# A scheduler that knows transfer rates and TensorE's clock, an urgency for every operation, and q in 64-row tokens

## The chip, the cores and the metric

The kernel runs on one core of one Trainium2 chip. The metric is the device time of one execution in microseconds (us); times are medians over runs of the same program. All arithmetic is on 32-bit floats (the MLP's matmuls take operands split into a high and a low part).

## The reference

One block: an adaptive layer norm, a gated long convolution, and a squared-ReLU MLP. S = 2048 tokens, D = 640 channels, F = 1728 hidden units.

```
mod = silu(c) @ w_mod                      # six rows of D: sa, ca, ga, sb, cb, gb
h  = layernorm(q) * (1 + ca) + sa
kv = causal_conv4(k, shift_k) * v          # 4 taps per channel
y  = causal_conv(kv, ssm_k) + kv * ssm_D   # 2048 taps per channel, by FFT
x  = q + ga * h * y
h  = layernorm(x) * (1 + cb) + sb
out = x + gb * (relu(h @ w1 + b1) ** 2 @ w2 + b2)
```

## The kernel before

**Two stages.** The first computes x, channel by channel, in NB = 5 batches of 128 channels. The second is the MLP over NC = 8 token tiles of 256 tokens.

**A batch b of the first stage.** `kv_load` brings k and v in (eight loads of 256 KB, written into tiles of KV), `kv` transposes them on TensorE, applies the four taps, multiplies, and stores kv to DRAM (`kv_d<-KV`); it is read back in another layout (`load_x`, `p<-kv_d`), beside ssm_k (`load_h`, `p<-in_A_ssm_k_dram`). The long convolution is a two-step Fourier transform by matmuls: `unit_a` (64x64 matmuls with the constant cw, `ps<-cst,p`), `spectra` (with the constant gb, `ps<-a,gb`), a complex product on DVE and POOL (`front`, tiles wx), `back` (with the constant gi), and `unit_y` (transposes, then the constant ca). In batch 0 the spectra of ssm_k are computed first (`early_h`). The epilogue of a batch is `load_xp` (q for these channels), `prep` (the norm of q, on ACT, DVE and POOL), and `finish`: tokens of MLP tiles 0 and 1 stay in SBUF, the others are summed on POOL and stored to DRAM (`x_d<-xp`). Statistics of q over all 640 channels are needed before the first epilogue: `q_stats` loads all of q once more, `stats1_end` finishes them. The modulation rows come from w_mod (25 loads, `wm<-in_w_mod_dram`, scaled on ACT and summed on POOL).

**The second stage.** Per token tile: load x (`load_x1`), statistics (`stats2`), normalise (`prep_hat`), transpose and split (`prep_xt`), then 14 blocks of F with `mlp_front` (x times w1), `mlp_middle` (bias, ReLU, square, split) and `mlp_back` (times w2, accumulated in four PSUM banks), and `mlp_out`. The weights are loaded once, during tile 0 and before (`w_load`: load, copy of the high part on ACT, low part on DVE).

**Token layout.** A partition of the first stage's result holds 16 neighbouring tokens: token = 64 n + 16 c + l lies at partition 32 c + n. So q's loads (`qsrc`) and the output's stores (`osrc`) go by four groups of 32 partitions.

**Who sets the order.** Nothing runs as written. Every operation becomes a node of a graph (`Graph`) with an engine, a cost in us, and the buffers it uses; nodes that belong together share a key, such as ("kn", 4) for batch 4's k and v loads. `levels` gives each node a priority: the longest path from it to the end plus a bias from the table `BIAS`, by kind or by kind and batch. `order` then plays the run forward: at each moment every engine takes the ready node of highest priority whose buffers are free, and a buffer is placed where it first fits. What comes out is one fixed order per engine, which `emit` writes down and `keep_order` pins. Loads and stores go out on SP's queue; `sp_issue` makes each wait for the fourth before it (OUT = 4), so that at most four are in flight. A DMA's time in the plan is `moved`: bytes per run of contiguous memory, one rate for all.

In the trace every operation recorded through the graph has line L375, and every SP load or store L564.

Of the kernel before, what the change touches and what calls it, by code (L numbers as in the profile page):

```python
# [13 lines left out]
AF = mybir.ActivationFunctionType  # L14
# [3 lines left out]
P = 128  # L18
# [5 lines left out]
NC = S // CH  # L24
EPS = 1e-5
OUT = 4

# [77 lines left out]


class Node:
    __slots__ = ("engine", "calls", "cost", "deps", "bufs", "entries", "dma", "id", "next", "prio", "key", "lock")  # L110


class Graph:
    def __init__(self):
        self.nodes, self.group, self.bufs = [], None, []
        self.key, self.bias = ("", 0), {}

    def buf(self, name, shape, dtype, choices, cell=32, line=None, psum=False):

# [85 lines left out]
    def order(self, lag=0.06, pelag=0.1, patience=0.0, trace=None):  # L205
# [55 lines left out]

        ready = {e: [] for e in ("PE", "ACT", "DVE", "POOL", "SP")}
        free = dict.fromkeys(ready, 0.0)
        soon = {e: [] for e in ready}
        need = [len(n.deps) for n in nodes]
        when = [0.0] * len(nodes)
        events = []
# [12 lines left out]
        while done < len(nodes):  # L280
            moved = False
            for e in ready:
                while free[e] <= t + 1e-9:
# [9 lines left out]
                            break  # L293
                    if pick is None:
                        break
                    if patience and e == "PE":
                        wait = [w for w, pr2, j in soon[e] if t < w < t + patience and pr2 < pr]
                        if wait:
                            heapq.heappush(events, (min(wait), -1))
                            break  # L300
                    n = nodes[ready[e].pop(pick)[1]]
                    for b, ci in got:
                        taken[b.n] = ci
                        for s in b.choices[ci][0]:
                            owner[s] = b.n
                    end = t + n.cost
                    if n.lock:
                        port = (end, e)
                    if e == "PE":
# [2 lines left out]
                            end = max(end, block + 4.0)  # L312
                            block, ent = end, ent - 256
                    if n.dma:
                        start = max(t + 1.4, dma_free)
                        dma_free = start + n.dma
                        land = dma_free + 0.7
                        heapq.heappush(events, (land, -1))
                        if e == "SP":
                            landed.append(land)  # L320
                        free[e] = t + n.cost
                        end = land
                    else:
                        free[e] = end
# [4 lines left out]
                    for i in n.next:  # L329
                        l = 0.0 if nodes[i].engine == e and not n.dma else pelag if e == "PE" else lag  # L330
                        when[i] = max(when[i], end + l)
                        need[i] -= 1
                        if not need[i]:
                            heapq.heappush(events, (when[i], i))
                            if patience:
                                soon[nodes[i].engine].append((when[i], -nodes[i].prio, i))
# [13 lines left out]
            while events and events[0][0] <= t + 1e-9:  # L350
                _, i = heapq.heappop(events)
                if i >= 0:
                    n = nodes[i]
                    bisect.insort(ready[n.engine], (-n.prio, i))
                    if patience:
                        soon[n.engine] = [x for x in soon[n.engine] if x[2] != i]
# [21 lines left out]
def _constants():  # L378
# [17 lines left out]
    for mm in range(1, 32):  # L396
# [27 lines left out]
    gt[0, :, 0] = gi.reshape(2, 64, 128).transpose(1, 0, 2)  # L424
    return {
        "cw": cw.astype(f),
        "ca": np.kron(np.eye(2), ca).astype(f),
        "gb": gb.reshape(128, 4096).astype(f),
        "gi": gt.reshape(128, 64, 2, 2, 16).swapaxes(3, 4).reshape(128, 4096).astype(f),
    }  # L430


# [1 line left out]
def ssm_mlp_kernel(  # L434
# [135 lines left out]
    def moved(o, i, run):  # L570
        x = o if isinstance(o, View) and o.ap is None else i
        n = (x.p[1] - x.p[0]) * x.ix.size * 4
        return n / run * (0.0095 + 4.1e-5 * run) / 16

    def sp_dma(o, i, run):
        g.add("SP", 0.4, (sp_issue, "dma", (o, i), {}), [x for x in (o,) if isinstance(x, View)],
              [x for x in (i,) if isinstance(x, View)], dma=moved(o, i, run))

    def act_dma(o, i, run):
        g.add("ACT", 0.06, (nc.scalar.dma_start, "dma", (o, i), {}), [x for x in (o,) if isinstance(x, View)],  # L580
              [x for x in (i,) if isinstance(x, View)], dma=moved(o, i, run))

    def cost(engine, op, args, kw):
# [89 lines left out]
    def mod_sum(j):  # L673
        ts = []
        for b in range(NB):
            t = stg(f"wm_{j}_{b}")
            ts.append(t)
            g.key = ("lm", j)
            sp_dma(t, w_mod[b * P : (b + 1) * P, j * D : (j + 1) * D], 2560)
            g.key = ("ms", j)  # L680
            act.activation(t, t, AF.Copy, scale=sg[:, b : b + 1])
            if b:
                add(pool, ts[0], ts[0], t)
        return ts[0]
# [34 lines left out]
    def q_stats(choices, l0, n, line=None):  # L719
        g.key = ("lq", l0)  # L720
        t = sbuf(f"q_{l0}", (P, n, D), choices, line=line)
        for a in range(4):
            sp_dma(t[32 * a : 32 * a + 32], qsrc[a, :, l0 : l0 + n], 2560)
        g.key = ("st1", l0)
        for i in range(n):
            dve_stats(st1[:, l0 + i], t[:, i])

    def stats1_end():
        g.key = ("st1e", 0)
        act.activation(rs1, st1[:, :, 1], AF.Sqrt, bias=eps_t)  # L730
        dve.reciprocal(rs1, rs1)
        dve.scalar_tensor_tensor(nm1, st1[:, :, 0], -1.0, rs1, op0=ALU.mult, op1=ALU.mult)


    gb = sbuf("gb", (P, 16, 2, 2, 64), [whole("S5")])
# [221 lines left out]
    def load_xp(b):  # L957
        g.key = ("lxp", b)
        t = XPt[b] = sbuf(f"xp_{b}", (P, NL, P), [whole(f"XP{b % 2}")])
        for a in range(4):  # L960
            sp_dma(t[32 * a : 32 * a + 32], qsrc[a, :, :, b * P : (b + 1) * P], 512)

    def prep(b, j):
        g.key = ("pra", b)
# [2 lines left out]
        u = U[b, j] = sbuf(f"u_{b}_{j}", (P, 4, P), UT if b < 2 else UT + up0 + up1 if b < NB - 1 else up0)  # L967
        for i in range(4):
            l = 4 * j + i
            act.activation(u[:, i], XPt[b][:, l], AF.Identity, scale=rs1[:, l : l + 1], bias=nm1[:, l : l + 1])  # L970
# [182 lines left out]
    def mlp_out(n):  # L1153
        g.key = ("out", n)
        for s in range(2):
# [7 lines left out]
            for i in range(2):  # L1163
                o = slice(i * 320, (i + 1) * 320)
                add(dve if s else pool, X1t[n][:, s, o], t[:, o], X1t[n][:, s, o])
                if s or i:
                    o = o if s else slice(0, D)
                    for a in range(4):
                        (act_dma if a % 2 else sp_dma)(
                            osrc[a, :, 2 * n + s, o], X1t[n][32 * a : 32 * a + 32, s, o], 2560  # L1170
                        )
        if n < NC - 1:
            for a in range(4):
                sp_dma(osrc[a, :, 2 * n : 2 * n + 2], X1t[n][32 * a : 32 * a + 32], 5120)

    BIAS = {
        "b1": 40, ("comb", 3): 40, "f2": -170, "fin": -160, ("fin", 0): -10, "gate": -185, "h": 40,
        ("h", 1): 215, "hat": 155, ("kn", 4): -25, ("ks", 0): 10, "kst": 335, ("kt", 3): 95, ("kt", 4): 60,
        ("lh", 3): -10, ("lh", 4): -15, ("lm", 1): 20, ("lm", 3): 40, ("mr", 1): -40, ("mr", 2): 15,
        ("mr", 4): 160, "mul": 40, ("mul", 2): 100, ("pa", 1): 60, "pac": -5, ("pac", 1): -55, ("pac", 2): 5,  # L1180
        ("pac", 3): 190, ("prm", 0): 40, "prp": -130, "qp": 490, ("qpc", 0): -5, ("st1", 10): 205, "tc": 225,
        ("vt", 2): -105, "wl": -240, ("wl", 6): -130, ("wl", 7): -85, ("x", 0): -10, "xt": 610, "y": -40,
        ("y", 0): -85, ("yc", 1): 90, ("yc", 4): 55,
    }

    KVB, PAB, XB, QB = ANY[::-1], ANY, ANY, ANY[2:6][::-1]
# [169 lines left out]
```

## Time and profile before

| | |
|---|---|
| median of three runs | 708.71 us (706.67 to 709.03) |
| the profiled execution | 712.65 us |
| its span, first to last instruction | 710.9 us |
| mean granted TensorE clock | 0.973 |
| PE busy | 650.5 us, 92% of the span |
| DVE, ACT, POOL busy | 381.3, 328.6, 253.1 us |
| moved by DMA | 74.46 MB |

The profile is of one execution, and its times are read against its own 712.65 us. A busy TensorE is not TensorE at its peak: a matmul at half clock counts as busy for twice as long. The engine that waits is not always the one that is late: a row names what released it.

### The profile page before, as it was taken

The numbers are of one execution on the slowest core, as the hardware profiler recorded it, in microseconds if no ns is written. First come the engines' busy times: TensorE is split into PE (matmuls) and PEld (weight loads), VectorE is DVE, ScalarE is ACT, GpSimd is POOL, SyncE is SP. The second block draws the span as 40 slices with busy tenths as digits, with TensorE's granted clock in tenths as the row PEclk, the third lists the DMA queues.
The fourth block names the chain that finished last, engine by engine and source line by source line (L and its number), as shares of the span: only waits on it lengthen the run. The fifth ranks groups of instructions, "written<-read, shape, count | busy, mean of one in ns | idle before, by whom it ended". The sixth has DMA issues, their size and how long they took to land.

```text
span 710.9 us, 17833 instructions
## 1 busy us (share of the span) xinstructions
PE 650.5 (92%) x7509; PEld 581.9 (82%) x7509; DVE 381.3 (54%) x780; ACT 328.6 (46%) x678; POOL 253.1 (36%) x316
## 2 busy tenths in 40 slices
PE   4968989789996899799999999999999999999996
PEld 3857867667785596479999999999999998998996
DVE  4545365567686667685235537456255356254451
ACT  3544657658877688465323324324124224233330
POOL 1126576336878287625401301203004004013010
PEclk9799999989998899999999999999999999999999
DMA  9888799799775761743002002001020020020011
GB/s 211 259 226 268 199 244 255 193 201 235 166 205 145 184 135 47 235 142 104 0 1 75 1 1 75 1 19 56 1 49 27 1 69 7 1 75 0 1 38 38
DMA packets 109125, 74.46 MB, mean 105 GB/s; under 512 B 49267, under 2 KB 96371, under 8 KB 108789
## 3 DMA queue, kind: packets, MB, share of 16 engines
q1 hardware_dynamic: 107088, 72.87, 39.2%
q8 instruction: 59, 0.97, 0.6%
q10 hardware_dynamic: 1892, 0.44, 0.3%
q14 instruction: 22, 0.17, 0.1%
q0 software_dynamic: 64, 0.01, 0.0%
HBM read 58.88 MB, written 14.42 MB: 103 GB/s over the span
## 4 chain that ended last, share of the span: by engine, by line
PE 69%; DMA 20%; DVE 5%; issue 2%; ACT 1%; SPq 1%; POOL 0%; DVEq 0%; ACTq 0%; POOLq 0%
PE ps L375 69%; DMA wm<-in_w_mod_dram 4%; DMA q<-in_A_q_dram 2%; DMA KV<-in_A_k_dram 2%; DMA kv_d<-KV 2%; DMA gb<-in_gb_dram 2%; DMA p<-kv_d 2%; DMA w2s<-in_B_w_dram 1%; DVE mtmp L375 1%; SPq L564 1%; DMA xp<-in_A_q_dram 1%; DVE KV L375 1%; DMA p<-in_A_ssm_k_dram 1%; DMA KV<-in_A_v_dram 1%; DVE s L375 1%
## 5 line engine op out<-in xcount | busy, mean ns | idle before, releaser
L375 PE MATMUL ps<-xt,w_S 128*128 128x512 f32 (+1 forms) x935 | 161.2, 328 | 0.9 <-ACT mtmp L375 0.9
L375 PEld LDWEIGHTS ps<-xt,w_S 128*128 128x128 f32 x935 | 139.2, 189 | 16.7 <-ACT mtmp L375 1.3
L375 PE MATMUL ps<-w_S,hring 128*128 128x320 f32 x648 | 106.3, 311 | 0.0
L375 PEld LDWEIGHTS ps<-w_S,hring 128*128 128x128 f32 x648 | 97.6, 188 | 0.7
L375 PE MATMUL ps<-a,gb 128*64 128x128 f32 x1280 | 81.8, 283 | 5.0 <-issue 1.3
L375 PEld LDWEIGHTS ps<-a,gb 128*64 128x64 f32 x1280 | 72.7, 141 | 14.6 <-issue 6.8
L375 ACT ACTIVATE hring<-mtmp 128x256 fp32r<-128x256 f32 x74 | 30.7, 416 | 112.2 <-PE ps L375 110.1
L375 POOL TENSOR_TENSOR x<-mtmp,x 128x640 f32<-128x640 f32 (+1 forms) x9 | 13.5, 1501 | 188.9 <-DVE mtmp L375 188.9
L375 ACT ACTIVATE mtmp<-ps,b1t 128x256 f32<-128x256 f32 (+1 forms) x112 | 51.8, 472 | 49.8 <-DVE hring L375 21.6
L375 POOL TENSOR_TENSOR wx<-wx 128x256 f32<-128x256 f32 x80 | 60.6, 777 | 25.5 <-DVE wx L375 23.5
L375 PE MATMUL ps<-cst,p 64*64 64x64 f32 x2560 | 51.4, 236 | 16.2 <-issue 8.3
L375 PEld LDWEIGHTS ps<-cst,p 64*64 64x64 f32 x2560 | 46.8, 149 | 21.3 <-issue 10.6
L375 DVE TENSOR_TENSOR hring<-mtmp,hring 128x256 fp32r<-128x256 f32 x74 | 34.1, 469 | 55.4 <-ACT hring L375 55.2
L375 DVE TENSOR_TENSOR mtmp<-ps,mtmp 128x256 f32<-128x256 f32 (+1 forms) x99 | 41.2, 420 | 39.6 <-ACT mtmp L375 39.5
L375 ACT ACTIVATE a<-ps 128x512 f32<-128x512 f32 x80 | 44.9, 629 | 25.7 <-PE ps L375 25.6
L375 POOL TENSOR_TENSOR x<-x,gb2row 128x640 f32<-128x640 f32 x16 | 25.1, 1586 | 82.7 <-ACT mtmp L375 51.9
L375 DVE TENSOR_TENSOR wx<-ps,wx 128x512 f32<-128x512 f32 x64 | 41.0, 684 | 24.3 <-PE ps L375 18.9
L375 PE MATMUL ps<-w_S,w_W 128*128 128x320 f32 x312 | 52.4, 311 | 0.3 <-DVE w_W L375 0.3
L375 ACT ACTIVATE w_W<-mtmp 128x256 fp32r<-128x256 f32 (+1 forms) x38 | 15.8, 417 | 71.5 <-PE ps L375 71.3
L375 PEld LDWEIGHTS ps<-w_S,w_W 128*128 128x128 f32 x312 | 47.0, 188 | 0.9 <-DVE w_W L375 0.5
L375 PE MATMUL ps<-gi,wx 64*128 64x128 f32 x640 | 41.0, 278 | 3.5 <-ACT q L375 3.3
L375 DVE SCALAR_TENSOR_TENSOR mtmp<-mtmp 128x256 f32<-128x256 f32 x91 | 42.8, 471 | 2.4
(128 smaller groups left out, 1031.7 us busy)
## 6 DMA issues: line engine op xcount, KB each, us to landing
wm<-in_w_mod_dram SPq DMA_DIRECT2D x25, 320.0 KB, 4.7
KV<-in_A_k_dram SPq DMA_DIRECT2D x20, 256.0 KB, 4.2
KV<-in_A_v_dram SPq DMA_DIRECT2D x20, 256.0 KB, 4.5
p<-in_A_ssm_k_dram SPq DMA_DIRECT2D x20, 256.0 KB, 4.6
p<-kv_d SPq DMA_DIRECT2D x20, 256.0 KB, 4.7
xp<-in_A_q_dram SPq DMA_DIRECT2D x20, 256.0 KB, 5.4
out_dram<-x SPq DMA_DIRECT2D x28, 160.0 KB, 2.6
w1s<-in_B_w_dram SPq DMA_DIRECT2D x13, 320.0 KB, 3.9
```

Of the source, the lines that this page charges most:

```text
L375: fn(*real, **{k: a.real() if isinstance(a, View) else a for k, a in kw.items()})
L564: nc.sync.dma_start(o, i)
```

## The change

Four things.

1. **The plan's rates.** `order` gives TensorE a clock that follows its own use: time is cut in windows of 10.24/3 us (from `phase`, 0), a window runs at half rate if the one before was used too little. DMAs get a rate by kind (`moved`: a factor 1.4 for transfers of at most 32 partitions and for those whose destination is in DRAM, 1.05 for the others), 1.2 us before and 1.0 us after the transfer instead of 1.4 and 0.7; a DMA issued on ACT costs ACT 0.4 us. The unused `patience` goes.
2. **An urgency per operation.** `BIAS` goes. A table `URGE` gives each node a number by its key and its turn within the key; the number takes the place of the path length. It covers the whole first stage, the weights, and token tiles 0 and 1. Nodes without an entry (token tiles 2 to 7) keep their path length, less 3000, without any bias.
3. **Tokens by 64 partitions.** token = 32 m + 16 h + l lies at partition 64 h + m. q's loads and the output's stores go by two groups of 64 partitions; the second of a batch's two q loads is issued on ACT's queue; the constants ca and gi are permuted to match.
4. **q's statistics by whole rows.** Partition p loads its 16 tokens 16 p to 16 p + 15, two at a time, over all 128 partitions (9 loads instead of 24). Two matmuls with every second column of the identity bring the statistics into the token layout.

```diff
-            n.prio = level[n.id] + self.bias.get(n.key[0], 0.0) + self.bias.get(n.key, 0.0)
+            n.prio = level[n.id]
+        turn = {}
+        for n in nodes:
+            i = n.nth = turn.get(n.key, 0)
+            turn[n.key] = i + 1
+            table = self.urge.get(n.key, ())
+            if i < len(table):
+                n.prio = table[i] / 10
+            elif self.urge:
+                n.prio -= 3000.0
...
+        def rate(k):
+            if k not in slow:
+                if k < 4:
+                    slow[k] = False
+                else:
+                    before = rate(k - 1) == 0.5
+                    u = util.get(k - 1, 0.0) / WINDOW
+                    slow[k] = u < 0.85 if before else u < 0.45
+            return 0.5 if slow[k] else 1.0
...
-                    end = t + n.cost
+                    end = run(t, n.cost) if e == "PE" else t + n.cost
...
-                        start = max(t + 1.4, dma_free)
+                        start = max(t + 1.2, dma_free)
                         dma_free = start + n.dma
-                        land = dma_free + 0.7
+                        land = dma_free + 1.0
...
-        return n / run * (0.0095 + 4.1e-5 * run) / 16
+        few = x.p[1] - x.p[0] <= 32
+        away = not isinstance(o, View) or o.ap is not None
+        return n / run * (0.0095 + 4.1e-5 * run) / 16 * (1.4 if few or away else 1.05)
...
-    qsrc = q.rearrange("(n c l) d -> c n l d", n=32, c=4)
-    osrc = out.rearrange("(n c l) d -> c n l d", n=32, c=4)
+    qsrc = q.rearrange("(m h l) d -> h m l d", m=64, h=2)
+    osrc = out.rearrange("(m h l) d -> h m l d", m=64, h=2)
+    qrow = q.rearrange("(p l) d -> p l d", p=P)
...
-        for a in range(4):
-            sp_dma(t[32 * a : 32 * a + 32], qsrc[a, :, l0 : l0 + n], 2560)
+        for i in range(0, n, 2):
+            e = min(i + 2, n)
+            sp_dma(t[:, i:e], qrow[:, l0 + i : l0 + e], 2560 * (e - i))
...
+        t = psum("stp", (P, NL, 2), ONE)
+        with g.as_one(0.3):
+            for h in range(2):
+                mm(t[64 * h : 64 * h + 64].rearrange("p l c -> p (l c)"), ident[:, h::2], st1.rearrange("p l c -> p (l c)"), True, True)
-        act.activation(rs1, st1[:, :, 1], AF.Sqrt, bias=eps_t)
+        act.activation(rs1, t[:, :, 1], AF.Sqrt, bias=eps_t)
...
-        for a in range(4):
-            sp_dma(t[32 * a : 32 * a + 32], qsrc[a, :, :, b * P : (b + 1) * P], 512)
+        for h in range(2):
+            (act_dma if h else sp_dma)(t[64 * h : 64 * h + 64], qsrc[h, :, :, b * P : (b + 1) * P], 512)
...
-            for a in range(4):
-                sp_dma(osrc[a, :, 2 * n : 2 * n + 2], X1t[n][32 * a : 32 * a + 32], 5120)
-    BIAS = {
-        "b1": 40, ("comb", 3): 40, "f2": -170, "fin": -160, ("fin", 0): -10, "gate": -185, "h": 40,
...
+            for a in range(2):
+                sp_dma(osrc[a, :, 2 * n : 2 * n + 2], X1t[n][64 * a : 64 * a + 64], 5120)
+    URGE = {
+        ("kn", 0): [-144, -133, -123, -113, -179, -226, -17, -154],
...
+        ("kn", 4): [-1541, -1530, -1561, -1582, -1692, -1743, -1753, -1823],
...
+        ("lh", 0): [-189, -229, -84, -129, -56, -102, -4, -54],
...
+        ("lq", 0): [-809, -777],
...
+        ("lq", 12): [-530, -962],
...
+        ("lw", 0): [-1602, -1764],
...
+        ("mul", 3): [-1807, -1814, -1827, -1820, -1878, -1865, -1894, -1901, -1922, -1915, -1953, -1960, -2042,
+            -2049, -2080, -2087],
...
-    g.bias = BIAS
+    g.urge = URGE
```

More of the change, by code (lines that the diff above doesn't have):

```diff
@@ L109 @@
 class Node:
-    __slots__ = ("engine", "calls", "cost", "deps", "bufs", "entries", "dma", "id", "next", "prio", "key", "lock")
+    __slots__ = ("engine", "calls", "cost", "deps", "bufs", "entries", "dma", "id", "next", "prio", "key", "lock", "nth")
 class Graph:
@@ L202, in levels, with order, run @@
             level[n.id] = top + n.cost + n.dma
-            n.prio = level[n.id] + self.bias.get(n.key[0], 0.0) + self.bias.get(n.key, 0.0)
-    def order(self, lag=0.06, pelag=0.1, patience=0.0, trace=None):
-        self.levels()
+            n.prio = level[n.id]
[8 more added lines that the diff above has]
+                n.prio -= 3000.0
+    def order(self, lag=0.06, pelag=0.1, phase=0.0):
+        self.levels()
+        util, slow = {}, {}
+        def rate(k):
[7 more added lines that the diff above has]
+            return 0.5 if slow[k] else 1.0
+        def run(t, work):
+            while work > 1e-9:
+                k = int((t + phase) / WINDOW)
+                for j in range(len(slow), k):
+                    rate(j)
+                room = (k + 1) * WINDOW - phase - t
+                r = rate(k)
+                step = min(room, work / r)
+                util[k] = util.get(k, 0.0) + step
+                work -= step * r
+                t = t + step if step < room else (k + 1) * WINDOW - phase + 1e-9
+            return t
         nodes, bufs = self.nodes, self.bufs
@@ L579, in act_dma @@
     def act_dma(o, i, run):
-        g.add("ACT", 0.06, (nc.scalar.dma_start, "dma", (o, i), {}), [x for x in (o,) if isinstance(x, View)],
+        g.add("ACT", 0.4, (nc.scalar.dma_start, "dma", (o, i), {}), [x for x in (o,) if isinstance(x, View)],
               [x for x in (i,) if isinstance(x, View)], dma=moved(o, i, run))
@@ L1176, in ssm_mlp_kernel @@
-    BIAS = {
-        "b1": 40, ("comb", 3): 40, "f2": -170, "fin": -160, ("fin", 0): -10, "gate": -185, "h": 40,
[L1178 to L1183, printed above, removed]
+            for a in range(2):
+                sp_dma(osrc[a, :, 2 * n : 2 * n + 2], X1t[n][64 * a : 64 * a + 64], 5120)
```

106 lines of the change are left out of this document (87 added, 19 removed), and 184 rows, old and new, of the table URGE.

## The prediction

> **What bounds the kernel now.** I read the page's parts on the span first, then the busy time by stretches, then the DMA queue's own instructions and waits, and last the chain that ended last. Span, work and clock come first:
>
> ```profile
> span 710.9 us, 17833 instructions
> PE   4968989789996899799999999999999999999996
> PEclk9799999989998899999999999999999999999999
> DMA  9888799799775761743002002001020020020011
> ```
>
> The digits cut the run in two. In the first 17 slices of 17.8 us (to about 306 us: the convolution, the gate by q, the first residual) TensorE has gaps, its clock dips, and the DMA engines are nearly full. Behind that (the MLP) TensorE stays at 9 and the DMA engines stand mostly idle. The same by stretches (length, then busy time of PE, its weight loads, DVE, ACT and POOL, the granted clock, the mean share of the DMA engines, GB/s):
>
> ```profile
> 0.00:80.00 80.00, 57.24 (x1453) 51.80 (x1454) 38.05 (x71) 37.27 (x69) 24.88 (x58) 0.91 0.89 235
> 80.00:183.00 103.00, 89.49 (x1615) 71.96 (x1613) 61.76 (x123) 67.95 (x128) 58.25 (x82) 0.93 0.91 226
> 183.00:306.00 123.00, 107.69 (x1876) 86.28 (x1877) 86.39 (x137) 88.09 (x179) 87.97 (x95) 0.96 0.59 153
> 306.00:711.00 405.00, 396.11 (x2569) 371.86 (x2567) 195.14 (x451) 135.24 (x305) 82.00 (x82) 1.00 0.12 34
> ```
>
> Call them A, B, C and D. In D TensorE is idle 8.9 of 405 us, so reordering can gain little there. In A to C it idles 22.8, 13.5 and 15.3 us. In A and B the DMA engines are 0.89 and 0.91 busy: TensorE waits for supply. In C they are at 0.59 and it waits all the same: that is order. The DMA queue's instructions say which order (start, us, what):
>
> ```profile
> 190.09 7.19 SPq L564 DMA_DIRECT2D x_d<-xp  x4
> 197.38 1.38 SPq L564 DMA_DIRECT2D KV<-in_A_k_dram  x1
> ...
> 256.01 1.93 SPq L564 DMA_DIRECT2D xp<-in_A_q_dram  x4
> 277.26 2.44 SPq L564 DMA_DIRECT2D x_d<-xp  x2
> ...
> 283.06 0.41 SPq L564 DMA_DIRECT2D w1s<-in_B_w_dram  x1
> ```
>
> Its waits (us in total, times, longest):
>
> ```profile
> SPq L564 <- POOL xp L375: 34.2, 9, 17.5
> ```
>
> The chain behind that k load, and TensorE's stretch around its end:
>
> ```profile
> 218.51 4.88 DMA kv_d<-KV
> ...
> 223.47 4.73 DMA p<-kv_d
> ...
> 228.34 3.96 PE ps L375 x158
> ```
>
> ```profile
> 220.00:240.00 20.00, 13.35 (x409) 11.02 (x402) 8.90 (x11) 11.45 (x21) 10.11 (x7) 0.74 0.61 160
> ```
>
> SP issues in order. Stores of the first residual (x_d<-xp) come to its head and wait for GpSimd's sum: 34.2 us in nine waits, the longest 17.5, inside the hole from 256.01 to 277.26. Batch 4's k load at 197.38 stands behind four such stores. From there a chain (k load, store of k times v, reload as p) runs to 228.34, and TensorE idles 6.65 us between 220 and 240 with the clock at 0.74. The hole before 277.26 does the same to the MLP's weights: the next goes out at 283.06.
>
> **The change, part by part.**
>
> *Half clock.* A mean clock of 0.91 over 80 us is (1 − 0.91) × 80 × 2 = 14.4 us at half rate; at A's busy share (57.24 of 80) half of the work in it is loss: 14.4 × 0.72 × 0.5 = 5.2 us. Likewise B 14.4 × 0.87 × 0.5 = 6.3, and C 9.8 × 0.88 × 0.5 = 4.3. The plan now counts with it; the chip gives it back only where TensorE's gaps close.
>
> *Loads of q.* SP keeps four DMAs in flight at most, so a kind's rate is four times its size over its time to land (the last column, us):
>
> ```profile
> wm<-in_w_mod_dram SPq DMA_DIRECT2D x25, 320.0 KB, 4.7
> KV<-in_A_k_dram SPq DMA_DIRECT2D x20, 256.0 KB, 4.2
> ...
> xp<-in_A_q_dram SPq DMA_DIRECT2D x20, 256.0 KB, 5.4
> ...
> q<-in_A_q_dram SPq DMA_DIRECT2D x8, 320.0 KB, 5.7
> ```
>
> The statistics' loads (5120 KB in 24 DMAs by 32 partitions, then in 9 over all 128) go at 4 × 320 / 5.7 = 225 KB per us; w_mod's rows, which fill 128 partitions, at 272. That is 22.8 against 18.8 us: 4.0 saved, all in B, where supply is the bound. The xp loads (5120 KB, by 32 partitions, then by 64) go at 190, at best at k's 244: 27.0 against 21.0 us, of which two batches of five lie in B, 2.4. I take the 2.4, as 64 is on the way to 128, and keep 0 for the range; xp loads in C count nothing, since the DMA engines have room there. [...] The rows of xp and k (5.4 and 4.2 for equal bytes) agree that few partitions are slow; none has 64.
>
> *Where work moves.* One xp load of each batch goes to ACT's queue, five issues in all, and the statistics' change of rows adds two matmuls. The nearest rows:
>
> ```profile
> 5.67 0.45 ACTq L375 DMA_DIRECT2D ct<-in_c_dram  x1
> ```
>
> ```profile
> L375 PE MATMUL ps<-ones,wm 128*128 128x1 f32 x20 | 2.6, 252 | 0.0
> ```
>
> Five times 0.45 us lie beside 193 us of ACT work in 306: hidden. If such an issue has to wait for its tile, ACT's copies out of PSUM stand behind it and TensorE waits for those; the nearest row is SP's wait, 0 to 17.5 us. I take 0: what waits for GpSimd there are the stores, and they stay on SP. The two matmuls are 0.5 us once, in TensorE's gaps. SP loses 30 loads and 14 stores of 0.3 to 0.5 us each; it is not the bound, so nothing, but about 1 us (0 to 3) at the very end, where the last tile's twelve issues become six. The permuted constants cost nothing: same instructions, same shapes.
>
> *Order.* Read as ranks, the new table puts things where the rows above want them: the loads of ssm_k and gb ahead of most of k and v of batch 0; the statistics' loads beside batch 0's products, ahead of most of batch 2's k and v; nearly all k and v loads of batch 4 and the first pair of MLP weights ahead of batch 3's products. The rows for what this can win:
>
> ```profile
> 7.51 6.37 PE L375 MATMUL ps<-ident,KV 128*128 128x128 f32 x32 [7.51 <-DMA KV<-in_A_k_dram]
> ```
>
> ```profile
> 123.76 6.42 DMA wm<-in_w_mod_dram
> 130.20 4.64 DMA q<-in_A_q_dram
> ```
>
> ```profile
> 280.00:300.00 20.00, 15.59 (x145) 10.65 (x144) 12.89 (x22) 9.95 (x17) 13.29 (x15) 1.00 0.68 210
> ```
>
> A: 22.8 idle, less the 7.5 until the first k has landed, plus 5.2 of clock: 20.5 are there. The DMA engines are at 0.89, so I take two fifths, 8 (0 to 15).
>
> B: 13.5 plus 6.3: 19.8 are there. The chain in it is loads of w_mod and q, which the batches' epilogues need. 6.4 come from the faster loads, and I put 5.6 on their coming earlier: 12 (4 to 17).
>
> C: 15.3 plus 4.3: 19.6 are there. Batch 4's stall is 6.65 idle and 0.26 × 20 × 2 × 0.67 × 0.5 = 3.5 of clock; the hole behind 280 is 4.4. With k, v and weights issued ahead of the stores these 14.5 go, and I put 1.5 on the rest: 16 (10 to 19). Late next are DVE and ACT, at 70 and 72% of C, and the epilogue of batch 4 itself.
>
> Sum: 8 + 12 + 16 + 1 = 37. The profiled execution took 712.65 us, 3.9 above the median of 708.71: 712.65 − 37 − 3.9 gives **672**. The ends, 14 and 54 us, give 695 and 655.
>
> **Rivals.**
>
> *Supply stays the bound (20%).* The order moves TensorE's waits about, but the bytes come no sooner: 4.0 to 6.4 us from the faster loads, and in C batch 4's 10. 708.7 − 15 = 694. For it: 0.89 and 0.91 in A and B, and equal bytes. Against it: 0.59 in C, and a tenth of A and B, 18 us, unused.
>
> *The clock's part does not come (12%).* The plan sets its clock windows from a fixed phase 0, so it may leave gaps where it thinks them harmless and they are not. Then the clock's 15.8 of all 59.9 stays away: 36 × 15.8 / 59.9 = 9.5 less, 681. For it: some 38 us at half rate in a front that idles only 51.6. Against it: B and C lose their longest gaps, and with them the dips. [...]
>
> *Stalls in every batch (11%, slower).* The plan is an order fixed beforehand with its slack taken out, and every engine runs it in order. If loads land later than its rates say, TensorE stands before the next batch's p, as it does now in batch 4, and all that is queued behind stands too: 6.65 and 3.5, 10 us a time. Three such stalls (batches 1 to 3), and of the gains only the 6.4 of the faster loads: 708.7 + 30 − 6.4 = 732. It decides from the first stall if no gain of order comes, from the fourth if all 37 do. For it: a store at SP's head already holds loads for 17.5 us, and xp is planned at a rate that no row shows. Against it: the new rates are nearer to the rows (few partitions slower) than one rate for all, and TensorE's waits for p are few in this trace:
>
> ```profile
> PE ps L375 <- DMA p<-kv_d: 6.4, 3, 3.0
> ```
>
> *The MLP's later tiles lose their place (7%).* The table ends with token tile 1; tiles 2 to 7 fall back to plain path length, without the old biases that pulled the next tile's tokens ahead (610 and 155). The chain through one such tile, and TensorE's stretch there:
>
> ```profile
> 583.40 4.06 DMA x<-x_d
> ...
> 593.81 110.92 PE ps L375 x709
> ```
>
> ```profile
> 580.00:600.00 20.00, 19.23 (x127) 17.88 (x126) 12.90 (x30) 8.15 (x19) 7.34 (x8) 1.00 0.21 59
> ```
>
> From the load of x to the first matmul on it are 10.4 us, now under the tile before, but for 0.77. If 3 us come bare in each of six tiles: 672 + 18 = 690.
>
> *The plan does not do what it says (2%).* Its new rates change nothing that the chip feels: 707 to 710.
>
> **How the numbers follow.** Forecast 48%, supply 20, clock 12, stalls 11, later tiles 7, nothing 2. Faster by over 0.3% (about what three runs from 706.67 to 709.03 can tell apart): 48 + 20 + 12 + 7, 0.87; same 0.02; slower 0.11. The range leaves out the stalls and some 3% each of the supply and later-tile cases above 702, and of the forecast below 650, near the sum of all that is there (712.65 − 3.9 − 59.9 − 1 = 648). The forecast's own range is 655 to 695.
>
> **What would show it.** Right: the MLP's first matmul near 270 us instead of 306; TensorE idle some 25 us up to there instead of 51.6; batch 4's k loads ahead of the x_d stores, and no dip of the clock at its p; statistics' loads landing in about 4.7 us per 320 KB and done by 110 us; D as long as now. Supply: PE digits of 7 and 8 all through the first ten slices under DMA digits of 9. Clock: as few gaps, but PEclk digits under 9. Stalls: PE waiting for p<-kv_d far over 6.4 us. Later tiles: PE digits under 9 behind 330 us. Wrong altogether: the idle time gone and the span as long, which would mean that the busy time itself is stretched.

## The result, and the profile after

The changed kernel takes **702.66 us** (median of 4 runs, 701.18 to 703.13) where the kernel before took 707.89 (706.67 to 709.03) beside it: ratio 0.9923, 95% interval 0.9898 to 0.9948, some 5 us faster. The forecast was 672, with a range of 650 to 702. The profiled execution took 702.44 us.

The page of the changed kernel, the same rows as before:

```profile
span 700.7 us, 17805 instructions
PE   3867998879988999899999999999999999999996
PEclk9999999998999999999999999999999999999999
DMA  9989889899885535542020020020020020110011
```

The cut between the two halves is where it was; the gaps and the full DMA engines of the first ten slices are still there. By stretches (length, then busy time of PE, its weight loads, DVE, ACT and POOL, the granted clock, the DMA engines' share, GB/s), the last row being the same MLP stretch as in the kernel before, from its first matmul on:

```profile
0.00:80.00 80.00, 55.90 (x1324) 49.39 (x1324) 39.04 (x73) 37.10 (x69) 27.37 (x55) 0.96 0.90 247
80.00:183.00 103.00, 91.31 (x1602) 74.91 (x1593) 71.36 (x137) 73.99 (x145) 65.81 (x87) 0.92 0.91 232
183.00:306.00 123.00, 113.86 (x2098) 93.84 (x2097) 87.85 (x131) 85.58 (x170) 83.86 (x98) 0.99 0.59 152
295.70:695.20 399.50, 396.09 (x2567) 373.05 (x2567) 199.25 (x454) 132.92 (x303) 80.19 (x81) 1.00 0.12 32
```

TensorE idles 24.1 us in A (22.8 before), 11.7 in B (13.5), 9.1 in C (15.3). The MLP takes 399.5 us as before (399.6, with the same 396 us busy). Its first matmul starts at 295.7 instead of 306.0, and these 10.3 us are the whole difference of the two profiles. The same view from the start to that matmul, the kernel before first:

```profile
0.00:306.00 306.00, 254.42 (x4942) 210.04 (x4943) 186.20 (x330) 193.31 (x374) 171.10 (x234) 0.94 0.78 199
0.00:295.70 295.70, 251.98 (x4947) 209.54 (x4947) 189.34 (x326) 193.48 (x375) 173.55 (x236) 0.96 0.79 206
```

For the same work TensorE is idle for 43.7 us instead of 51.6 and busy for 252.0 instead of 254.4. What TensorE and SP wait for, three rows of the changed kernel (us in total, times, longest):

```profile
PE ps L402 <- issue: 16.1, 11, 2.4
PE ps L402 <- DMA KV<-in_A_k_dram: 7.4, 4, 4.9
SPq L591 <- POOL xp L402: 26.0, 5, 18.3
```

The wait for p<-kv_d, which held batch 4, is no longer among TensorE's ten largest. What has grown from the kernel before to this one is "issue": TensorE waits for nothing that the profile shows. All of it lies ahead of the MLP (4.9, 6.7 and 4.6 us in A, B and C). The same view of the kernel before had it at the top as well, and the prediction did not read it:

```profile
PE ps L375 <- issue: 12.3, 11, 2.9
```

The loads of q in the changed kernel (count, KB, us to land):

```profile
q<-in_A_q_dram SPq DMA_DIRECT2D x7, 640.0 KB, 7.2
xp<-in_A_q_dram SPq DMA_DIRECT2D x5, 512.0 KB, 6.8
xp<-in_A_q_dram ACTq DMA_DIRECT2D x5, 512.0 KB, 6.3
```

640 KB in 7.2 us is 356 KB per us with four in flight, against the 225 of the kernel before.

### The profile page after: what moved, and what is told of

Read it like the earlier page. It is cut to its first block, busy times and chain, and to the rows that moved or that the text cites. A ratio compares the mean times of both kernels' runs of the same rounds, so it can differ in the third digit from the quotient of the medians.

```text
span 700.7 us, 17805 instructions
## 1 busy us (share of the span) xinstructions
PE 648.1 (92%) x7513; PEld 582.6 (83%) x7513; DVE 389.4 (56%) x780; ACT 326.4 (47%) x678; POOL 253.8 (36%) x316
## 4 chain that ended last, share of the span: by engine, by line
PE 84%; DMA 6%; issue 3%; DVE 3%; ACT 2%; POOL 1%; SPq 0%; DVEq 0%; ACTq 0%; POOLq 0%
PE ps L402 84%; DMA p<-in_A_ssm_k_dram 2%; DMA KV<-in_A_k_dram 2%; DMA KV<-in_A_v_dram 1%; DVE KV L402 1%; DMA gb<-in_gb_dram 1%; DMA kv_d<-kacc 1%; ACT a L402 1%; DVE up L402 1%; DVE xt L402 0%; ACT KV L402 0%; POOL xt L402 0%; DVE wx L402 0%; SPq L591 0%; POOL x L402 0%
## 5 line engine op out<-in xcount | busy, mean ns | idle before, releaser
L402 PE MATMUL ps<-xt,w_S 128*128 128x512 f32 (+1 forms) x935 | 177.4, 331 | 3.6 <-POOL xt L402 1.6
L402 PEld LDWEIGHTS ps<-xt,w_S 128*128 128x128 f32 x935 | 142.8, 190 | 18.2 <-POOL xt L402 2.1
L402 PE MATMUL ps<-w_S,hring 128*128 128x320 f32 x648 | 109.0, 310 | 0.0
L402 PEld LDWEIGHTS ps<-a,gb 128*64 128x64 f32 x1280 | 74.6, 144 | 14.7 <-issue 5.9
L402 PE MATMUL ps<-a,gb 128*64 128x128 f32 x1280 | 83.5, 286 | 3.2 <-DVE wx L402 2.0
L402 PE MATMUL ps<-cst,p 64*64 64x64 f32 x2560 | 50.0, 229 | 23.3 <-issue 12.2
L402 PEld LDWEIGHTS ps<-cst,p 64*64 64x64 f32 x2560 | 44.6, 142 | 31.1 <-issue 14.2
L402 DVE TENSOR_TENSOR hring<-mtmp,hring 128x256 fp32r<-128x256 f32 x74 | 37.3, 510 | 53.3 <-ACT hring L402 52.8
L402 POOL TENSOR_TENSOR wx<-wx 128x256 f32<-128x256 f32 x80 | 58.5, 750 | 16.5 <-DVE wx L402 12.2
L402 DVE TENSOR_TENSOR wx<-ps,wx 128x512 f32<-128x512 f32 x64 | 41.1, 680 | 17.3 <-PE ps L402 15.0
L402 POOL TENSOR_TENSOR mtmp<-mtmp 128x256 f32<-128x256 f32 (+1 forms) x21 | 14.5, 690 | 83.8 <-ACT mtmp L402 83.5
L402 POOL TENSOR_TENSOR xt<-xfs,xt 128x256 fp32r<-128x256 f32 x35 | 28.3, 816 | 42.6 <-ACT xt L402 42.5
```

Source lines behind the costliest of these rows:

```text
L402: fn(*real, **{k: a.real() if isinstance(a, View) else a for k, a in kw.items()})
```

## The experiments

Theories. *Supply*: TensorE in A and B waits for bytes, whatever the order. *Plan*: the bytes are there, the fixed order and its wrong prices make TensorE wait. *Instructions*: TensorE's own program comes too slowly. All times are medians. The runs were made in four sets after that of the result, each with the kernel before beside them, and the ratio is to it. It took 710 to 714 us in these sets and 708 in that of the result, while the changed kernel took 701 to 703 wherever it ran. What moves the kernel before stays open. Runs of different sets are compared by their ratios, and a difference that their medians do not show as well is not taken for one.

**After as it is (twice).**

> The changed kernel as it is, beside the three that follow, on their chip. The kernel before took 707.9 us on the chip of the result and 713.0 on that of the first four experiments, a change between chips (or hours) of 0.7%, as large as what is to be told apart. If the changed kernel moves with it, its ratio stays at 0.992; if the two orders meet such a change differently (the changed one plans with the clock), the ratio moves: 0.986 would be 702.7 against 713.

> The changed kernel as it is, as the measure for the three others of this call: 702 to 704 us, as on the three occasions so far.

703.18 us, ratio 0.9846 [0.9812, 0.9881], and 701.09, 0.9821 [0.9787, 0.9855]. It is the kernel before that moved: the gain is 5 us in the result and 9 to 13 here.

### Loads or order?

**Old order, new loads.**

```diff
-            sp_dma(t[32 * a : 32 * a + 32], qsrc[a, :, l0 : l0 + n], 2560)
+            sp_dma(t[32 * a : 32 * a + 32], qold[a, :, l0 : l0 + n], 2560)
+            i, e = 2 * a, min(2 * a + 2, n)
+            instead(*([(sp_issue, (t[:, i:e], qrow[:, l0 + i : l0 + e]))] if i < n else []))
...
```

`instead` replaces what a planned operation issues and leaves its place; xp and the stores are replaced likewise.

> The kernel before with its order kept instruction by instruction, but the statistics' loads by whole rows, xp loads and stores by 64 partitions (two in the place of four), all on SP as before; the change of rows of the statistics is left out. My prediction's term: 6.4 us of faster loads, 701 to 703 us. With xp by 64 partitions no faster than by 32: 4.0, 704. If a DMA's rate here does not depend on its partitions, or B is not bound by supply: 707 to 709, no change.

704.38 us, 0.9877 [0.9833, 0.9922]: the loads alone, in an order that was never planned for them, bring 8.8 us.

**Old order, only the statistics' loads by whole rows.** The edit above without its part for xp and the stores.

> The kernel before in its order, with the statistics' loads alone by whole rows (the change of rows left out); xp and the stores stay by 32 partitions. With both kinds of load changed this order gained 8.6 us (704.4 against 713.0). My prediction's split was 4.0 for the statistics and 2.4 for xp, so 5 to 6 of the 8.6 here, ratio 0.992. If xp and the stores by 64 partitions brought the most of it, under 3 us, 0.996 or above. If they brought nothing, all 8.6: 0.988.

705.40 us, 0.990 [0.9873, 0.9928]: 7.2 us (5.1 to 9.0). xp and the stores by 64 partitions add nothing that these intervals resolve.

**New order, old loads.**

```diff
             sp_dma(t[:, i:e], qrow[:, l0 + i : l0 + e], 2560 * (e - i))
+            instead(*((sp_issue, (t[32 * a : 32 * a + 32, i:e], qold[a, :, l0 + i : l0 + e])) for a in range(4)))
...
```

> The changed kernel in its order, but q is loaded and stored by 32 partitions, as before (two DMAs in the place of one for xp and the stores, 36 of 160 KB for the statistics where before had 24). If the gain of 5.2 us is the order's (batch 4's stall and the hole ahead of the weights), it stays: 701 to 704 us. If it is the loads', it goes: 706 to 710. If the order needs the faster loads because its plan counts on them, it is slower than the kernel before: over 710.

713.97 us, 1.0013 [0.9983, 1.0043]: without its loads the order brings nothing (the statistics have 36 small loads here, where the kernel before had 24; what that costs was not measured).

**Loads alone, one kind after the other.** Three of the six kinds:

```
load(t[32 * a : 32 * a + 32], q32[a, :, :, b * P : (b + 1) * P])      # cols32
load(t[64 * h : 64 * h + 64], q64[h, :, :, b * P : (b + 1) * P])      # cols64
load(t[:, 2 * i : 2 * i + 2], q128[:, 2 * i : 2 * i + 2])             # whole128
```

> No part of the computation: only loads on SP, four in flight, one kind after the other, each from the tensor that the kernels read (then stores of zeros as output). Kinds: 256 KB of k by 128 partitions in pieces of 512 B (rows128); q by 32 partitions, 256 KB, and by 64, 512 KB, in pieces of 512 B (cols32, cols64); ssm_k by 128 partitions in pieces of 256 B (short128); q by 32 partitions, 320 KB, pieces of 10 KB (whole32), and by 128, 640 KB, pieces of 5 KB (whole128). My prediction: cols64 nearer to rows128's rate than to cols32's. [...] If a DMA's partitions do not matter, all three in pieces of 512 B go at the same KB per us.

```profile
whole<-in_A_q_dram SPq DMA_DIRECT2D x8, 640.0 KB, 6.2
cols<-in_A_q_dram SPq DMA_DIRECT2D x8, 512.0 KB, 9.7
rows<-in_A_k_dram SPq DMA_DIRECT2D x12, 256.0 KB, 3.7
cols<-in_A_q_dram SPq DMA_DIRECT2D x12, 256.0 KB, 5.0
whole<-in_A_q_dram SPq DMA_DIRECT2D x8, 320.0 KB, 5.9
short<-in_A_ssm_k_dram SPq DMA_DIRECT2D x8, 256.0 KB, 5.0
```

Four in flight, so 4 x KB / us: whole rows by 128 partitions go at 413 KB per us, by 32 at 217, nearly twice. In pieces of 512 B it is 277 by 128 partitions, 205 by 32, and 211 by 64: 64 partitions are no better than 32. Partitions do not decide alone: ssm_k, by 128 partitions in pieces of 256 B, goes at 205 as well.

**The two halves on two queues.**

```diff
-load(t[64 * h : 64 * h + 64], q64[h, :, :, b * P : (b + 1) * P])
+load(t[64 * h : 64 * h + 64], q64[h, :, :, b * P : (b + 1) * P], ("SP", "ACT")[h], 2)
```

> Only loads again. First q by 64 partitions, 512 KB in pieces of 512 B, all on SP with four in flight (one64; alone this went at 211 KB per us), then the same with partitions 0 to 63 on SP and 64 to 127 on ACT's queue, two in flight on each (two64), then k by 128 partitions, 256 KB, in turn on SP and ACT (tworows; on SP alone 277 KB per us). [...]

```profile
one<-in_A_q_dram SPq DMA_DIRECT2D x10, 512.0 KB, 9.7
two<-in_A_q_dram SPq DMA_DIRECT2D x5, 512.0 KB, 8.5
two<-in_A_q_dram ACTq DMA_DIRECT2D x5, 512.0 KB, 9.7
```

211 KB per us on one queue; 2 x 512 / 8.5 + 2 x 512 / 9.7 = 226 on two. The halves do not add up, and k's rows by 128 partitions gained nothing from two queues either: they landed in 4.6 and 4.1 us, 236 KB per us against 277 on one. That 64 partitions are as slow as 32 is measured, why is not.

### Do bytes bound the changed kernel?

**A fifth of the statistics' bytes.**

```diff
             sp_dma(t[:, i:e], qrow[:, l0 + i : l0 + e], 2560 * (e - i))
+            g.nodes[-1].calls[-1] = (sp_issue, "dma", (t[:, i:e, 0:128], qrow[:, l0 + i : l0 + e, 0:128]), {})
...
```

The added line replaces what the planned load issues.

> The changed kernel in the same order of instructions, but each load of q for the statistics brings 128 of its 640 columns (4096 of 5120 KB left out; the statistics are taken over those columns alone). Supply theory (stretches A and B wait for bytes, whatever the order): 4096 KB at the 232 GB/s of stretch B are some 17 us of DMA time, of which I expect 6 to 12 to reach the end, 690 to 697 us, with TensorE's idle time in 80 to 183 us falling from 11.7 to under 6. Plan theory (the bytes are there in time, the fixed order and its wrong rates keep TensorE waiting): under 3 us, 700 to 703, the idle time as it is.

696.97 us, 0.9775 [0.9735, 0.9816]: 5.0 us less than the changed kernel by the ratios (0.9846; 3.3 by 0.9821), below the 6 to 12 that supply foresaw for some 17 us of freed DMA time and above the 3 of plan. TensorE's gaps did not close (14.2 us idle in B; the granted clock there is 0.97 instead of 0.92), and the issue gaps hardly moved:

```profile
80.00:183.00 103.00, 88.81 (x1768) 71.83 (x1764) 67.79 (x140) 78.31 (x158) 72.38 (x98) 0.97 0.90 213
```

```profile
PE ps L402 <- issue: 14.8, 13, 2.4
```

**Eight in flight.**

```diff
-        if len(queued) > OUT:
+        if len(queued) > 8:
...
```

> The changed kernel in the same order, but SP keeps up to eight DMAs in flight instead of four. Supply theory, DMA engines full: no change, 701 to 704 us, each DMA simply takes twice as long from issue to landing. Supply theory, but four in flight are too few to fill the engines: the shares of 0.90 and 0.91 rise to 0.95 or more and 3 to 8 us go, 695 to 700. Plan theory: within 2 us either way, since what is late is late by order and not by the queue's depth.

702.56 us, 0.9855 [0.9811, 0.9899]: no difference from the changed kernel, which plan and full DMA engines both foresaw. In its profile the first 80 us were a little fuller, as they should be if four in flight were too few, and nothing of that was left at the end (stretch A, then a wait):

```profile
0.00:80.00 80.00, 60.83 (x1420) 53.81 (x1424) 42.75 (x82) 41.30 (x77) 30.68 (x61) 0.96 0.95 263
```

```profile
PE ps L402 <- issue: 18.8, 13, 3.5
```

The DMA engines rise to 0.95 in A (0.90, 0.91 and 0.94 in three profiles of the changed kernel) and TensorE is busy for 60.8 us (55.9, 58.1, 59.7), both just above what these three show. The issue gaps are no shorter (16.1, 16.3 and 18.1 us there), and the MLP's first matmul starts at 295.2 us instead of 295.7.

### TensorE's instructions

The issue gaps have a pattern. The timeline of PE in the changed kernel (start, us, operation, count, and in brackets the idle time before):

```profile
190.20 0.80 PE L402 MATMUL ps<-cst,p 64*64 64x64 f32 x38 [1.25 <-issue]
190.94 2.06 PE L402 MATMUL ps<-gi,wx 64*128 64x128 f32 x32
192.92 1.08 PE L402 MATMUL ps<-cst,p 64*64 64x64 f32 x57
195.54 0.34 PE L402 MATMUL ps<-cst,p 64*64 64x64 f32 x7 [1.53 <-issue]
195.81 1.97 PE L402 MATMUL ps<-a,gb 128*64 128x128 f32 x32
197.71 1.51 PE L402 MATMUL ps<-cst,p 64*64 64x64 f32 x88
199.87 0.81 PE L402 MATMUL ps<-cst,p 64*64 64x64 f32 x40 [0.66 <-issue]
```

From gap to gap are 38 + 32 + 57 = 127 and 7 + 32 + 88 = 127 matmuls, with their weight loads 254 instructions; they take 5.3 and 4.3 us. The counts hold for the rest of this profile: up to the first gap 128 matmuls, then 473, 254, 126, 508, 508, 507 and 636, and 890 from the last gap shown to the next one. All but the 473, which ends in a gap of 0.3 us, are one to seven times some 127. So the program of TensorE comes in blocks of 256, and the next is not there yet. The rows of the instruction queue, in the last section, agree on the size: 59 packets of 16 KB (0.97 MB) for the 2 x 7513 matmuls and weight loads of the changed kernel, 255 to a packet, and 49 for the 2 x 6233 of the next experiment, 254 to a packet. 128 of the MLP's matmuls take 399.5 / 2567 x 128 = 19.9 us, so no block is late there. 128 of the convolution's first product (ps<-cst,p, 50.0 us for 2560 in the front) take 2.5 us: where they stand bunched, a block is late, as in the 5.3 and 4.3 us above. The planner has a price for it, 4.0 us (`end = max(end, block + 4.0)` in `order`, in both kernels), below the 4.3 and 5.3 read here.

**Half the instructions in that product.**

```diff
+                            c = g.group.calls.pop()
+                            if r == 0:
+                                z, y = 64 * (j % 2), j - j % 2
+                                o = t[e][z : z + 64, y : y + 2].rearrange("p j m d -> p (j m d)")
+                                g.group.calls.append((c[0], c[1], (o, c[2][1], cst[l, 0:128]), c[3]))
```

> The changed kernel with the same plan, but the first product of the convolution (ps<-cst,p, 2560 matmuls of 64 columns in 64x64 tiles) done as 1280 of 128 columns: the same columns streamed, half the instructions; its sums land in other places, so the values are not the convolution's. TensorE's gaps put down to issue come mostly every 126 to 128 of these matmuls, which is 256 instructions with the weight loads. Instruction theory (TensorE's instructions come in blocks of 256, and one block takes 4 to 6 us when the DMA engines are busy): the 16.1 us of issue gaps fall below 8, and 5 to 12 us reach the end, 690 to 698. Supply theory: the gaps turn into waits for loads, under 3 us, 700 to 703.

**685.61 us**, 0.9612 [0.9584, 0.964]: 17.6 us less than the changed kernel beside it.

```profile
span 685.5 us, 15248 instructions
PE   3878996799889999899999999999999999999996
PEclk9999999999999999999999999999999999999999
DMA  9989999999985618350020200020020110110011
```

```profile
L402 PE MATMUL ps<-cst,p 64*64 64x128 f32 x1280 | 45.3, 285 | 13.1 <-POOL p L402 10.0 <-DMA p<-kv_d 1.6 <-issue 0.7
```

That group's issue gaps are 0.7 us, against 12.2 in the same group of the changed kernel and 16.1 on all of TensorE. PEclk is 9 throughout. Its matmuls also got 4.7 us shorter in all, which explains a part of the 17.6. The MLP's first matmul starts at 281.2 us instead of 295.7; up to it TensorE is busy for 244.8 us instead of 252.0 and idle for 36.4 instead of 43.7. So the idle time fell by less than half of the issue gaps that went: other waits took the rest (one for ACT's q alone is 4.8 us).

**The same edit in the kernel before.**

> The kernel before in its order, with the first product of the convolution in 1280 matmuls of 128 columns instead of 2560 of 64 (the sums land in other places, so the values are not the convolution's). In the changed kernel this brought 17.6 us. Instruction theory, and the kernel before bound by it as well: its issue gaps were 12.3 us, so 8 to 18 us, ratio 0.975 to 0.989. If the kernel before was bound by its loads instead and the instruction blocks came to bind only when the loads were made faster: under 4 us, 0.995 or above.

706.28 us, 0.9953 [0.9922, 0.9985]: only 3.3 us, so the issue gaps alone did not bind the kernel before. Without them the old order and loads wait for something else, k and ACT's copies:

```profile
PE ps L375 <- DMA KV<-in_A_k_dram: 12.8, 4, 7.3
PE ps L375 <- ACT q L375: 10.1, 7, 4.1
```

**The square completed.** The same edit in the two kernels that mix order and loads.

> The kernel before in its order, with the loads of the change (whole rows for the statistics, 64 partitions for xp and the stores; the statistics' change of rows left out) and the first product in half as many matmuls (sums in other places). New order and new loads with half the instructions took 685.6 us, ratio 0.961; old order and old loads 0.995; old order and new loads at full instructions 0.988. If the faster loads uncover the instruction bound whatever the order: 0.962 to 0.970. If the order's gain was hidden behind the instruction blocks: 0.980 to 0.986, loads and instructions adding up (0.988 x 0.995 = 0.983).

> The changed kernel's order with q loaded and stored by 32 partitions as before, and the first product in half as many matmuls (sums in other places). At full instructions this order with these loads was no faster than the kernel before, 1.001. If the order's gain was hidden behind the instruction blocks and needs no faster loads: 0.970 to 0.982. If it needs both: 0.988 to 0.998.

692.98 us, 0.9717 [0.9684, 0.975], and 699.51 us, 0.9805 [0.9771, 0.9839]. All ratios, each with an interval of 0.25 to 0.45% either way in its own set of runs:

| | all instructions | half in the first product |
|---|---|---|
| old order, old loads | 1 | 0.9953 |
| old order, new loads | 0.9877 | 0.9717 |
| new order, old loads | 1.0013 | 0.9805 |
| new order, new loads | 0.9923, 0.9846, 0.9821 | 0.9612 |

With half the instructions the order is worth 1.5% with the old loads and 1.05% with the new (10.5 and 7.5 us of 712), the loads 2.4 and 1.9% (17 and 14 us), and they nearly add up. With all instructions the order is worth nothing with the old loads and 0.3 to 0.6% with the new (nothing by the result's 0.9923), the loads 1.2 to 1.9%. The cells come from different sets, and the changed kernel's own ratio differs by 1% between them. The medians without the kernel before say the same: with half the instructions the order is worth 6.8 and 7.4 us and the loads 13.3 and 13.9; with all of them the order is worth 1 to 3 us with the new loads and nothing with the old. So the order's gain exists, and TensorE's instruction supply hides most of it.

### What the plan knows

**Old rates, no clock in the plan.**

```diff
-                    end = run(t, n.cost) if e == "PE" else t + n.cost
+                    end = t + n.cost
...
-        return n / run * (0.0095 + 4.1e-5 * run) / 16 * (1.4 if few or away else 1.05)
+        return n / run * (0.0095 + 4.1e-5 * run) / 16
...
```

> The changed kernel with its table of urgencies and its loads, but the planner's old rates (one for all DMAs, 1.4 and 0.7 us around them) and no clock of TensorE in the plan; the order that comes out differs. Its own plan says 669.2 us, the changed kernel's 669.1. If the rates and the clock in the plan carry a part of the gain: 705 to 709. If the plan lacks what really binds (the instruction blocks) in both: 701 to 705, no difference that can be measured. Played forward with 5.3 to 5.8 us per block it is 3 us longer than the changed kernel's order, so I expect 704 to 706.

705.19 us, 0.9921 [0.9885, 0.9956]. The changed kernel did not run in this set. By the ratios of the later sets (0.9846, 0.9821) this is 5 to 7 us behind it, by the medians 2 to 4, and by the result's 0.9923 level with it. How much of the gain the rates and the clock in the plan carry is not settled.

**A table searched against the blocks (twice).** Most numbers of the table differ; two of its lines (in the changed kernel and here):

```diff
-        ("lxp", 0): [-985, -902],
-        ("lq", 0): [-809, -777],
+        ('lxp', 0): [-636.51316, -359.8781],
+        ('lq', 0): [-850.52517, -828.13233],
```

> The changed kernel with another table of urgencies and nothing else. The table comes from a search over the changed one: each order is played forward a second time, fixed, with 5.3 to 5.8 us per 256 TensorE instructions instead of the planner's 4.0, and with DMAs 0 to 10% slower. Played so, the changed kernel's order takes 697.3, 692.3 and 700.7 us (span on the chip: 700.7), this one's 692.1, 687.8 and 693.3. Instruction theory: the chip gives back most of the mean difference of 5.7 us, 696 to 699 against 703, ratio to the kernel before near 0.978, fewer issue gaps than 16 us. If the order can't do anything about the blocks: 702 to 704. If the table is tuned to details that the chip does not have: slower, 705 to 712.

> The kernel with the table that was searched against 5.3 to 5.8 us per instruction block, again, now beside the changed kernel. It took 700.6 us where the kernel before took 710.3, the changed kernel 703.2 against 712.6 and 702.6 against 713.0 (deep queue) on other occasions. If the search is worth what the replay says, 4 to 6 us less than the changed kernel in this call; if the 2.5 us seen is all, 1 to 4; if it was chance, within 1.

700.63 us, 0.9853 [0.9805, 0.99]; then 699.35, 0.9815 [0.9773, 0.9857], beside the changed kernel's 701.09. The 1.7 us lie within the spread of its runs (696.57 to 705.21), and the issue gaps stayed (17.3 and 16.8 us). The replay promised 5.7. An order that beats the changed kernel is not shown: this new order did not bring the blocks any sooner.

## Why the prediction was wrong

The sign and the place were right (the front, not the MLP), the size was not: 37 us were summed; 10 came between the two profiles, and 5 to 13 between the medians that ran beside each other. The steps, each as the prediction put it:

- **"There to be won" is the step that failed.** It took TensorE's idle time and its half clock, 59.9 us in A to C, for time that an order can fill. It went by the DMA share alone: where the engines were full, supply; where not, order. It left out the top row of TensorE's own waits, issue 12.3 us, for which neither is the reason. The square shows the consequence: the order's 7 to 10.5 us appear only when the instructions are halved. That step does not hold all that is missing: with half the instructions on both sides the whole change is worth 21 us by the medians and 24 by the ratios, so some 13 to 16 of the 37 would not have come even then. Of these the 2.4 for xp are accounted for below; the cause of the rest stays open.
- **A, 8 us.** The clock rose from 0.91 to 0.96, worth 0.05 x 80 x 2 x 0.7 x 0.5 = 2.8 us; idle time rose by 1.3. So 1.5, and 4 to 5 by the other two profiles of this kernel, which were busier there. The two fifths that were taken came from no row.
- **B, 12 us.** Idle time fell by 1.8, the clock went from 0.93 to 0.92 and took some 0.9 back. So 0.9, and 1.4 and -0.6 in the other two profiles. The statistics moved forward as foreseen (their last load is issued at 103.5 us, their square root on ACT runs at 118.2 instead of 151.0), but gaps of issue came in B instead (6.7 us, where the kernel before had 1.5).
- **Loads of q, 6.4.** Both terms were mis-sized. The statistics' 4.0 had w_mod's 272 KB per us as its upper row; alone, whole rows by 128 partitions go at 413 against 217, 11.2 us of DMA time, and 7.2 us arrived in the old order. xp's 2.4 was taken because 64 is on the way to 128. It is nothing: 211 against 205 KB per us.
- **C, 16 us.** The mechanism was right: batch 4's k loads went out at 170 to 194 us, ahead of most of the stores, the dip at its p is gone, and idle time fell by 6.2 us and the clock from 0.96 to 0.99 gave 0.03 x 123 x 2 x 0.9 x 0.5 = 3.3. So 9.5, in part because the last 10 us of this stretch are now the MLP's; in the other two profiles the clock is 0.96 and 0.97, which leaves 5.5 and 6. SP still stands 18.3 us behind one sum of GpSimd.
- **D, 1 us.** None: 399.5 against 399.6.

Of the rivals, *the plan does not do what it says* (707 to 710) lay nearest by its number, by luck: the loads did land faster and batch 4's stall did go. *Supply stays the bound* (694) came nearest by its mechanism: the DMA engines are as full in A and B as before (0.90 and 0.91; the bytes per us rose by 5 and 3%), and the loads brought more than the order. It missed the second supply: leaving out four fifths of the statistics' bytes won 5 us, halving one product's instructions 17.6. *Stalls in every batch* and *later tiles* did not happen: p<-kv_d has left the large waits, and the MLP is as long as it was. Of *the clock's part*, 15.8, a third came by the granted clock in this profile (2.8 - 0.9 + 3.3) and 3 to 4 us in the other two; by TensorE's busy time for the same work it was 2.4 us (0.6 and 2.2 in the others).

What would have brought the forecast nearer from the profile before alone: the issue row, 12.3 us in 11 gaps, and the count of matmuls between them. Taken off the 59.9 it would not have put it right.

## What to carry to other kernels

Before idle time on an engine is counted as room for a better order, split it by what ended it, and read "issue" as a resource of its own: count the instructions between such gaps, and where the count is constant (here some 127 matmuls, 254 instructions), the program itself is what is late. A run of short matmuls (here 20 ns each) is then priced by its number, not by its columns; making half as many, twice as wide, was worth 17.6 us in the changed kernel, more than the whole change, and 3.3 in the kernel before, where loads and order bound as well. And two edits that each look worthless or small alone may be hidden behind the same third bound: a square with that bound taken away shows it.

## What the runs showed of the hardware

Blocks of 256 TensorE instructions came 4.3 and 5.3 us apart while the DMA engines were at 0.95:

```profile
186.30:200.00 13.70, 10.18 (x415) 9.35 (x419) 7.62 (x13) 10.04 (x23) 12.99 (x19) 1.00 0.95 237
```

The blocks are DMAs themselves, on a queue of their own; with half of one product's matmuls it is ten fewer, 2560 instructions (first the changed kernel, then that experiment; packets, MB):

```profile
q8 instruction: 59, 0.97, 0.6%
```

```profile
q8 instruction: 49, 0.80, 0.5%
```

What sets the 4 to 5 us was not settled: eight data DMAs in flight instead of four left the issue gaps just above their spread (18.8 us against 16.1 to 18.1), and fewer than four were not tried. A load's rate followed its shape by a factor of two: 413 KB per us for whole rows over 128 partitions, 205 for 512 B pieces over 32 and for 256 B pieces over 128.

The granted clock had two levels, 1.00 and 0.50. Before the MLP it stood at 0.50 for 10.2, 3.4, 3.4, 6.8, 3.4, 6.8 and 3.4 us in the kernel before, 37.6 us in all, and for five times 3.4 and once 6.8 in the changed one, 23.9. These are multiples of the plan's window of 10.24 / 3 us; its limits for a slow window, 0.45 and 0.85, no run tested. Each of these stretches came behind idle time on TensorE, 0.7 to 4.0 of the 4 us ahead of it, but 2.6 idle of the 3 us from 35.5 in the kernel before were followed by none. In the kernel before, 32 matmuls of ps<-a,gb (128x128) took 3.68 us at 0.50 and 1.97 at 1.00; those of ps<-cst,p (64x64) took 30 ns each at 0.50 and 18 to 19 at 1.00. So half clock made them 1.5 to 1.9 times as long, not twice, and the clock terms of the prediction and of the section on why it was wrong, which take half of the work for loss, are upper estimates.
